# A Mamba2 scan with an ELU feed-forward layer on one core: where B's decay factor comes from, when block three and four are summed, and a last store in pieces

## The chip, the cores and the metric

The kernel runs on one core of a Trainium2 chip. The metric is the device time of one execution in microseconds (us), as the median of several executions. The core has these engines: PE (TensorE: matrix products, and PEld for its loads of weights), DVE (VectorE), ACT (ScalarE), POOL (GpSimd) and SP (SyncE, which here only issues DMAs). Each engine works through its own list of instructions in order and waits by semaphores for the others.

## The reference

Two computations follow each other. The first is a state-space scan (Mamba2), for 4 sequences of 768 tokens, 8 heads of width 32, and a state of width 16. For one chunk of tokens:

```python
cum = cumsum(log(clip(a, 1e-6, 1)))            # within the chunk
L   = exp(cum[:, None] - cum[None, :]) * causal
y   = (C @ B.T * L) @ x  +  (C @ state) * exp(cum)
state = exp(cum[-1]) * state + (B * exp(cum[-1] - cum)).T @ x
```

The heads of a token are then joined to a row of 256, which gives 3072 rows, and a feed-forward layer follows, `elu(y @ w_in) @ w_out`, from 256 to 2048 and back to 256. All is float32.

## The kernel before

**Blocks.** The 3072 tokens are cut into 12 blocks of 256, numbered n = 0 to 11 in the code. Block n is one third of one sequence. In the words of the change "block three" is n = 2 and "block four" is n = 3; below, blocks go by their n. In a block the scan works with four chunks of 64 tokens, written (u, v) with u and v in 0 and 1.

**The scan of a block.** `spread_cum(n)` (L348) loads the running sums from a table in DRAM that the kernel wrote before (`write_flat`), spread over the partitions. The exponential of these differences, by ACT (`decay_of` and `decay`, L481, with the token's own sum, `ncum`, as the bias), followed by POOL's causal select (L486), is the tile L: for a token j in the partition, a head, u, and a token i in the row, exp(cum_i - cum_j). Its last column, i = 63, is thus exp(cum_last - cum_j), the factor by which B is scaled before it is summed into the state. Before the change that factor is made on its own: `rest_of_sums` (L317) takes the differences to the last token on POOL (L299) and their exponential on ACT, and `turned` transposes it on PE and copies it on DVE to a tile `eb` (L961). `scaled(n)` (L374, the product is L379) multiplies B by it, on POOL; blocks 0 and 1 read an own tile eb0.

The rest of the scan is a list of steps with these lines. `turn` transposes B and C. `scores` (L501) multiplies C and B on PE, in four PSUM banks; `weigh` (L510) multiplies a bank by L on DVE and gives M. `sums` (L531) multiplies the scaled B and x on PE; `states` makes from it the state of each chunk on DVE (S_new, L548) and from each of these a masked copy on POOL (Sx, L553). `across` (L576, C by Sx) and `inside` (L595, M by x) are PE's products of block n's output y, which ACT copies to the tile yT (L612). In between, `ec`, the tile of exp(cum), is needed for C and for the states. Blocks 0 to 2 get it from `first_exp(n)` (L364: a product that picks heads by a mask from `make_heads`, L277, on POOL, and a copy on ACT), blocks 3 on from `spread_exp(n)` (L357), one load of 128 KB from a table in DRAM.

**The feed-forward layer.** `l1(n, i)` (L627) is the first product for block n and the i-th 256 of 2048 columns; with a second argument `parts` it is cut along the tokens, so that PE makes twice as many passes of half the width. `elu` follows it: e on ACT (L640), its exponential on ACT (L647), and g on DVE (L649), which frees the PSUM bank of the product. The products take turns in a pool of seven PSUM banks (an eighth is kept apart, p_o). `l2` (L748) is the second product for blocks 0 and 1. The weights come in 16 pieces (0 to 7 of w_in, 8 to 15 of w_out) of 512 KB. For a piece, `w_take` and `w_give` convert the words that the load brought: L174 (on ACT), L183, L192, L200 and L207 (on DVE), L217 (on POOL). A load of a piece is issued five or six pieces ahead.

From block 4 on, two blocks are worked on together. The products are combined from seven products of quarters in place of eight (`front`, `mid` and `back`, L699 to L732; `second`, L809, with sums of the products in L800, in c_sum). `second(n)` runs over two halves of the columns and over seven products r = 0 to 6 in each; `store(n, at)` (L852) writes one of the two blocks, 256 KB.

**The order.** Nothing schedules: what each engine does, and in which order, is the order in which the Python code calls these functions. Four stretches of it matter here.

- The start (L900 to L965): the first weights, blocks 0 and 1, and the first loads.
- A loop of twelve l1 for blocks 0 and 1, with s = 0 to 11 (L968 to L1006). Beside it run the decays of block 2 (s < 8), weight pieces 5 to 9 (at odd s), and the steps of block 2.
- Two rounds of eight l1 for n = 2 and 3, with i = 0 to 7 (L1087 to L1123). Beside them run the second products of blocks 0 and 1, pieces 10 to 15, and the scan of block 3; `scan_ahead(n, i)` (L1021) adds steps for blocks 4 and 5, and later for the blocks two ahead.
- The pairs from n = 4 on (L1127 to L1199), and the tail for blocks 10 and 11 (L1201 to L1212).

In the second of these, block 2 goes like this:

```python
        if s == 8:
            ...
            weigh(2, 2)
            weigh(2, 3)
            ...
            sums(2, 0, pool=p_o, tag="o", parts=(None, last))
            states(0, last)
            ...
            states(2)
        if s == 10:
            spread_cum(4)
            inside(across(2), 2)
```

Of the kernel before, what the change touches and what calls it, by code (L numbers as in the profile page):

```python
# [28 lines left out]
def kernel(  # L29
# [72 lines left out]
    def rows_of(n):  # L102
        b, g = place(n)
        return slice(NG * NH * b + g, NG * NH * (b + 1), NG)
# [165 lines left out]


    heads = [const.tile([P, NH, N], F32, name=f"heads{n}") for n in range(2)]
    heads.append(heads[0])

    def make_heads(n):
        cols = slice(BH + NH * n, BH + NH * (n + 1)) if n < 2 else rows_of(n)
        nc.gpsimd.tensor_copy(  # L277
            heads[n], ident[:, cols].unsqueeze(2).to_broadcast([P, NH, N]))

# [32 lines left out]
    nc.scalar.activation(E0, E0, ACT.Exp)  # L312

    F = const.tile([ROWS, 2, 2, P], F32, name="F")
    E = la

    def rest_of_sums():  # L317
        to_last(F[:, 0], E, nc.gpsimd)
        nc.scalar.activation(E, E, ACT.Exp)


    flat = tc.dram_tile([2, ROWS, 2, Q], F32, name="flat")
# [41 lines left out]
    def first_exp(n):  # L364

        ps = psum([P, 2, P], "ps_ec")
        rows = P if n < 2 else ROWS
        nc.tensor.matmul(
            out=ps, lhsT=heads[n][0:rows].rearrange("p h n -> p (h n)"),
            rhs=la0 if n < 2 else F[:, 1], start=True, stop=True)  # L370
        st[n]["ec"] = att.tile([P, 2, P], F32, tag="ec", name="ec", bufs=4)
        nc.scalar.copy(out=st[n]["ec"], in_=ps)

    def scaled(n, eng):  # L374

        s = st[n]
        s["sc"] = sc = att.tile([P, 2, NH, N], F32, tag="sc", name="sc", bufs=2)
        factor = eb0[:, :, NH * n:NH * (n + 1)] if n < 2 else eb[:, :, rows_of(n)]
        eng.tensor_tensor(  # L379
            out=sc, in0=s["b"] if n > 3 else s["bc"][:, 0],  # L380
            in1=factor.unsqueeze(3).to_broadcast([P, 2, NH, N]), op=ALU.mult)
# [91 lines left out]
    def decay(n, q):  # L473

        decay_of(n, 2 * q)
        decay_of(n, 2 * q + 1)
# [306 lines left out]

    c_of = {}

    def second(n):


        c = c_of[n] = ffn.tile([P, 2, 2, 2, P], F32, tag="c", name="c_sum", bufs=1)
        c11, c12, c21, c22 = (c[:, at, :, e] for e in range(2) for at in range(2))  # L790
        a11, a12, s1, a22 = a_out
        s2, s3, s4 = s_out
        for half in range(2):
            tmp = ffn.tile([P, 3, 2, P], F32, tag="tmp", name="p_sum", bufs=1)
            p1, p5, u = (tmp[:, r] for r in range(3))
            chunk = range(4 * half, 4 * half + 4)

            def add(out, in0, in1):
                eng = nc.vector if in0.tensor is ps.tensor else nc.gpsimd
                eng.tensor_tensor(out=out, in0=in0, in1=in1, op=ALU.add)  # L800

            for r, a in enumerate((a11, a12, s1, s2, s3, a22, s4)):
                pool, tag = (p_a, "a") if (7 * half + r) % 2 else (p_o, "o")
                ps = pool.tile([P, 2, P], F32, tag=tag, name="ps_o")
                for i in chunk:
                    b11, b21, b12, b22 = quarters(n, i)
                    b = (b11, b21, b12, t2_of[n, i], b11, b21, b22)[r]
                    for ts in range(2):
                        nc.tensor.matmul(  # L809
                            out=ps[:, ts], lhsT=b[:, ts * P:(ts + 1) * P], rhs=a[:, i],  # L810
                            start=(i == chunk[0] and ts == 0), stop=(i == chunk[-1]),
                            skip_group_check=True)
                    if i < chunk[-1]:
                        yield
                if r == 0:
                    nc.scalar.copy(out=p1, in_=ps)
                    for i in chunk:
                        b11 = quarters(n, i)[0]
                        sub(b11, t2_of[n, i], b11)
                    if half:  # L820
                        add(c11, c11, p1)
                elif r == 1:
                    add(c11, ps, c11 if half else p1)
                    for i in chunk:
                        b21 = quarters(n, i)[1]
                        sub(b21, b21, t2_of[n, i])
                elif r == 2:
                    nc.scalar.copy(out=p5, in_=ps)
                elif r == 3:
                    add(u, ps, p1)  # L830
                    add(p5, p5, u)
                    if half:
                        add(c22, c22, p5)
                        add(c12, c12, p5)
                elif r == 4:
                    add(c22, ps, c22 if half else p5)
# [86 lines left out]
    nc.scalar.activation(F[:, 1], F[:, 0], ACT.Exp)  # L923
    write_flat()
    spread_cum(2)
    w_load(5)
    load_bc(2)
    w_load(6)
# [11 lines left out]
    turn(1)  # L940
    first_exp(1)
    scaled(1, nc.gpsimd)
    rest_of_sums()
    w_give(3)
    make_heads(2)
    turn_exp(1)
    l1(0, 2)
    elu()
# [9 lines left out]
    inside(across(1), 1)  # L958
    w_take(4, nc.vector)
    ncum = turned(F[:, 0], "ncum", -1.0, nc.vector)  # L960
    eb = turned(E, "eb", 1.0, nc.vector)  # L961
    w_give(4)
    elu()
    load_bc(3)
# [3 lines left out]
    for s, (n, i) in enumerate((  # L968
            (1, 0), (1, 1), (1, 2), (0, 4), (1, 3), (0, 5), (1, 4), (0, 6), (1, 5), (0, 7),
            (1, 6), (1, 7))):  # L970
        l1(n, i, 2 if s < 2 else 1)
        if s < 8:
            decay_of(2, s)
        if s == 7:
            scores(2)
            weigh(2, 0)
            weigh(2, 1)
        if s % 2 == 1 and todo < 10:
            w_take(todo, nc.vector)
            w_give(todo)  # L980
            w_load(todo + 6)
            todo += 1
        if s == 4:
            scaled(2, nc.gpsimd)
        if s == 5:
            turn(2)
            first_exp(2)
            turn_exp(2)
        if s == 8:
            spread_cum(3)  # L990
            load_x(3)
            spread_exp(3)
            weigh(2, 2)
            weigh(2, 3)

            st[0] = kept
            sums(2, 0, pool=p_o, tag="o", parts=(None, last))
            states(0, last)
            st.pop(0)
            states(2)  # L1000
        if s == 10:
            spread_cum(4)
            inside(across(2), 2)
        if len(lag) > 1:
            elu()
# [15 lines left out]
    def scan_ahead(n, i):  # L1021
# [6 lines left out]
        if 4 <= m < NP and n % 2 == 0:  # L1028
            if i < 2:
                if m == 4:  # L1030
                    load_bc(m + i)
                spread_exp(m + i)
            if i == 2:
                if m == 4:
                    spread_cum(5)
                load_x(m)
                load_x(m + 1)
            for k in (i,) if m == 4 else (i, i + 1) if i % 2 == 0 else ():
                if k >= 2:
# [11 lines left out]
        if 4 <= m < NP and n % 2 == 1:  # L1051
            if i == 0:
                scaled(m, nc.gpsimd)
                scaled(m + 1, nc.gpsimd)
            for k in (i,) if m == 4 else (i, i + 1) if i % 2 == 0 else ():
                if k < 2:
                    decay(m + 1, k + 2)
            if i == 2 and m == 4:
                scores(m, m + 1)
                sums(m, m + 1)  # L1060
                for q in range(4):
                    weigh(m, q)
                    weigh(m + 1, q)
                states(m)
                states(m + 1)
# [21 lines left out]
    for n in (2, 3):  # L1087
        for i in range(8):
# [13 lines left out]
            if n == 2:  # L1102
# [3 lines left out]
                if i == 1:  # L1106
                    scaled(3, nc.gpsimd)
                    turn(3)
                    turn_exp(3)
                if i == 2:  # L1110
                    scores(3)
                    for q in range(4):
                        weigh(3, q)
                if i == 4:
                    sums(3)
                    states(3)
                if i == 6:
                    inside(across(3), 3)
# [80 lines left out]
    next_elu()  # L1199

    n = NP - 2  # L1201
    steps = second(n)
    for k in range(56):
        if k == 1:
            store(n - 2, 0)
            store(n - 2, 1)
        if k == 54:
            store(n, 0)
        next(steps)
    for _ in steps:  # L1210
        pass
    store(n, 1)  # L1212


# [28 lines left out]
```

## Time and profile before

| | |
|---|---|
| median of 3 executions | 357.79 us (357.79 to 358.67) |
| the profiled execution, its own time | 357.64 us |
| its span in the profile | 355.9 us |
| granted clock of PE, mean | 0.998 |
| DMA | 26.36 MB, mean 74 GB/s |
| L809, PE's second products of pairs (`w_out` by g), 640 passes | 81.0 us, mean 275 ns |
| L627, PE's `l1`, 272 passes | 60.9 us, mean 371 ns |
| L699, PE's products of pairs (yT by `w_in`), 128 passes | 38.8 us, mean 385 ns |
| L640 and L647, ACT's e, 96 of each | 57.0 and 60.9 us, means 593 and 635 ns |
| L649, DVE's g, 96 | 65.1 us, mean 679 ns |
| L486, POOL's causal select, 40 | 28.8 us, mean 719 ns |

The first two times are of whole executions; the span is from the first to the last instruction that the profiler saw, and so a little shorter than the execution that it belongs to. A row of a chain or of an order in time starts with the start and the length in us; then come engine, line, operation, the tile written and the tiles read (out<-in), their sizes, a count where equal instructions are drawn together, and in brackets the idle time of the engine before it and what ended that. An engine may be busy for most of the span and still bound nothing: what sets the time is the chain of work that ends last.

### The profile page before, as it was taken

The numbers are of one execution on the slowest core, as the hardware profiler recorded it, in microseconds if no ns is written. First come the engines' busy times: TensorE is split into PE (matmuls) and PEld (weight loads), VectorE is DVE, ScalarE is ACT, GpSimd is POOL, SyncE is SP. The second block draws the span as 40 slices with busy tenths as digits, with TensorE's granted clock in tenths as the row PEclk, the third lists the DMA queues.
The fourth block names the chain that finished last, engine by engine and source line by source line (L and its number), as shares of the span: only waits on it lengthen the run. The fifth ranks groups of instructions, "written<-read, shape, count | busy, mean of one in ns | idle before, by whom it ended". The sixth has DMA issues, their size and how long they took to land.

```text
span 355.9 us, 9943 instructions
## 1 busy us (share of the span) xinstructions
PE 349.0 (98%) x3962; PEld 313.4 (88%) x3962; DVE 242.5 (68%) x500; ACT 200.5 (56%) x491; POOL 231.8 (65%) x367
## 2 busy tenths in 40 slices
PE   8899999999999999999999999999999999999995
PEld 5579888888888999899999899999899999999995
DVE  3999987993999768674677684677674555656212
ACT  4759969867425577535577535576635544444000
POOL 5553643663676997869477769477769444464973
PEclk9999999999999999999999999999999999999999
DMA  8978998470460500146500145600000100000001
GB/s 156 209 195 155 246 318 174 96 122 31 72 139 2 120 0 3 19 98 132 113 0 2 17 102 112 133 3 0 2 2 4 59 3 0 2 0 33 29 2 60
DMA packets 82742, 26.36 MB, mean 74 GB/s; under 512 B 59720, under 2 KB 78600, under 8 KB 82696
## 3 DMA queue, kind: packets, MB, share of 16 engines
q1 hardware_dynamic: 80520, 25.53, 32.2%
q8 instruction: 31, 0.51, 0.6%
q10 hardware_dynamic: 2176, 0.20, 0.5%
q14 instruction: 15, 0.12, 0.1%
HBM read 22.38 MB, written 3.34 MB: 72 GB/s over the span
## 4 chain that ended last, share of the span: by engine, by line
PE 93%; DVE 3%; ACT 1%; POOL 1%; issue 0%; POOLq 0%; DVEq 0%
PE ps_o L809 35%; PE ps_h L699 28%; PE ps_h L627 14%; PE ps_o L748 8%; PE ps_y L595 2%; PE ps_g L501 2%; PE ps_y L576 1%; PE ps_st L531 1%; PE ps_idle L232 1%; DVE mag L207 1%; DVE mag L200 1%; DVE M L510 1%; DVE sgn L192 0%; DVE g L649 0%; POOL w_in L217 0%; ACT L L471 0%
## 5 line engine op out<-in xcount | busy, mean ns | idle before, releaser
L640 ACT ACTIVATE e<-ps_h 128x512 f32<-128x512 f32 x96 | 57.0, 593 | 89.5 <-DVE ps_h L724 44.0
L809 PEld LDWEIGHTS ps_o<-w_out,g 128*128 128x128 f32 x640 | 79.9, 192 | 3.1 <-issue 0.5
L809 PE MATMUL ps_o<-w_out,g 128*128 128x128 f32 x640 | 81.0, 275 | 0.0
L649 DVE SCALAR_TENSOR_TENSOR g<-e,ps_h 128x512 f32<-128x512 f32 x96 | 65.1, 679 | 10.5 <-ACT e L647 10.4
L627 PE MATMUL ps_h<-yT,w_in 128*128 128x256 f32 (+1 forms) x272 | 60.9, 371 | 1.7 <-POOL w_in L217 1.7
L647 ACT ACTIVATE e<-e 128x512 f32<-128x512 f32 x96 | 60.9, 635 | 2.0
L776 POOL TENSOR_TENSOR g<-g 128x256 f32<-128x256 f32 x33 | 23.9, 726 | 54.4 <-DVE g L649 54.4
L627 PEld LDWEIGHTS ps_h<-yT,w_in 128*128 128x128 f32 x272 | 48.4, 190 | 9.5 <-POOL w_in L217 3.1
L809 PE MATMUL ps_o<-w_sum,g 128*128 128x128 f32 x320 | 42.9, 275 | 0.0
L809 PEld LDWEIGHTS ps_o<-w_sum,g 128*128 128x128 f32 x320 | 41.1, 192 | 1.2
L481 ACT ACTIVATE L<-L,ncum 128x64 f32<-128x64 f32 x160 | 41.0, 337 | 0.0
L699 PE MATMUL ps_h<-yT,w_in 128*128 128x256 f32 x128 | 38.8, 385 | 0.0
L732 DVE TENSOR_TENSOR ps_h<-ps_h,u_sum 128x512 f32<-128x512 f32 x32 | 22.3, 698 | 23.5 <-PE ps_h L699 23.4
L699 PE MATMUL ps_h<-y_sum,w_in 128*128 128x256 f32 x128 | 38.1, 380 | 0.0
L699 PE MATMUL ps_h<-y_sum,w_sum 128*128 128x256 f32 x128 | 38.1, 380 | 0.0
L486 POOL TENSOR_SCALAR_AFFINE_SELECT L<-L 64x512 f32<-64x512 f32 x40 | 28.8, 719 | 10.8 <-ACT L L481 9.5
L716 DVE TENSOR_TENSOR u_sum<-ps_h,u_sum 128x512 f32<-128x512 f32 x32 | 22.1, 689 | 14.5 <-ACT u_sum L709 8.1
L724 DVE TENSOR_TENSOR ps_h<-ps_h,u_sum 128x256 f32<-128x256 f32 x32 | 13.8, 432 | 26.3 <-PE ps_h L699 26.3
L748 PE MATMUL ps_o<-w_out,g 128*128 128x256 f32 x128 | 30.8, 384 | 0.0
L764 POOL TENSOR_TENSOR t<-g 128x256 f32<-128x256 f32 x40 | 28.9, 756 | 0.3
L764 POOL TENSOR_TENSOR g<-g,t 128x256 f32<-128x256 f32 x40 | 28.8, 752 | 0.3
L764 POOL TENSOR_TENSOR g<-t,g 128x256 f32<-128x256 f32 x40 | 27.9, 730 | 1.1 <-PE ps_o L809 1.1
(111 smaller groups left out, 533.9 us busy)
## 6 DMA issues: line engine op xcount, KB each, us to landing
L<-flat SPq DMA_DIRECT2D x20, 256.0 KB
w<-in_moe_w_in_dram SPq DMA_DIRECT2D x8, 512.0 KB
w<-in_moe_w_out_dram SPq DMA_DIRECT2D x8, 512.0 KB
xr<-in_x_dram SPq DMA_DIRECT2D x24, 128.0 KB
out_dram<-c_sum SPq DMA_DIRECT2D x10, 256.0 KB
bc<-in_B_dram SPq DMA_DIRECT2D x24, 64.0 KB
bc<-in_C_dram SPq DMA_DIRECT2D x22, 64.0 KB
ec<-flat_exp SPq DMA_DIRECT2D x9, 128.0 KB
```

The source lines that it names most:

```text
L481: nc.scalar.activation(L[:, h, u], L[:, h, u], ACT.Exp, bias=ncum[:, u, row:row + 1])
L486: nc.gpsimd.affine_select(out=part, in_=part, pattern=[[0, 4], [0, 2], [1, Q]], compare_op=ALU.is_ge, fill=0.0, base=0, channel_multiplier=-1)
L627: nc.tensor.matmul(out=ps[:, j, toks], lhsT=w_in[:, k, m * P:(m + 1) * P], rhs=yT[n // 2][:, k, n % 2].rearrange("p u i -> p (u i)")[:, toks],
L640: nc.scalar.activation(begun[0], lag[0][2], ACT.Relu, scale=-1.0)
L647: nc.scalar.activation(e, e, ACT.Exp, scale=-1.0)
L649: nc.vector.scalar_tensor_tensor(out=g_of[n, i], in0=e, scalar=1.0, in1=ps, op0=ALU.subtract, op1=ALU.max)
L699: nc.tensor.matmul(out=out, lhsT=lhsT, rhs=rhs, start=first, stop=True, skip_group_check=True)
L732: nc.vector.tensor_tensor(out=c2, in0=c2, in1=u[:, 0:2], op=ALU.add)
L748: nc.tensor.matmul(out=o_of[n][:, ts], lhsT=g_of[n, j][:, m % 2, ts * P:(ts + 1) * P], rhs=w_out[:, m], start=(m == 0 and ts == 0), stop=( ...
L764: nc.gpsimd.tensor_tensor(out=out, in0=in0, in1=in1, op=ALU.subtract)
L776: eng.tensor_tensor(out=b12, in0=b12, in1=b11, op=ALU.subtract)
L809: nc.tensor.matmul(out=ps[:, ts], lhsT=b[:, ts * P:(ts + 1) * P], rhs=a[:, i], start=(i == chunk[0] and ts == 0), stop=(i == chunk[-1]), s ...
```

## The change

- **The factor of B.** `rest_of_sums`, the tile `eb` and its transposes go. `scaled(n)` for n from 2 on reads `L[:, :, :, Q-1]`. `scaled(2)` moves from s = 4 to s = 7, behind the last decay.
- **ec of block 2.** `first_exp(2)` and the mask `make_heads(2)` go; `spread_exp(2)` is loaded, issued on SP right behind `spread_cum(2)` and ahead of weight piece 5, B and C of block 2, piece 6, x of block 2, and pieces 7 to 9.
- **Block 2.** `sums(2)` and the states move from s = 8 to s = 9, where they come behind `w_take(9)` and `w_give(9)` in the code; `inside(across(2))` moves from s = 10 to s = 11. The l1 at s = 2 is cut in halves, as those at s = 0 and 1 were.
- **Block 3.** `scores(3)` (before at i = 2) and `sums(3)` (before at i = 4) stand together at i = 3, ahead of `weigh`. The states stay at i = 4.
- **Later blocks.** `decay` comes two steps earlier for the pairs from m = 6 on, so that L is there for `scaled`; for block 5 `scaled` comes one step later.
- **The tail.** In the last half of `second(10)` the last of seven products is cut in two along the tokens. Each half has a PSUM tile, a sum of 128x128 on DVE, and a store of 64 KB of its own. The other 128 KB of block 11 are stored at k = 53, together with the store of block 10 (before at k = 54); the store of all of block 11 at the end goes.

```diff
-    heads.append(heads[0])
     def make_heads(n):
-        cols = slice(BH + NH * n, BH + NH * (n + 1)) if n < 2 else rows_of(n)
+        cols = slice(BH + NH * n, BH + NH * (n + 1))
...
-    E = la
-    def rest_of_sums():
-        to_last(F[:, 0], E, nc.gpsimd)
-        nc.scalar.activation(E, E, ACT.Exp)
...
     def scaled(n, eng):
-        factor = eb0[:, :, NH * n:NH * (n + 1)] if n < 2 else eb[:, :, rows_of(n)]
+        factor = (eb0[:, :, NH * n:NH * (n + 1)] if n < 2 else
+                  s["L"][:, :, :, Q - 1].rearrange("p h u -> p u h"))
...
     def second(n, final=False):
...
             for r, a in enumerate((a11, a12, s1, s2, s3, a22, s4)):
+                if final and half and r == 6:
+                    for ts in range(2):
+                        ps = psum([P, P], "ps_o")
+                        for i in chunk:
+                            nc.tensor.matmul(
+                                out=ps, lhsT=quarters(n, i)[3][:, ts * P:(ts + 1) * P],
+                                rhs=a[:, i], start=(i == chunk[0]), stop=(i == chunk[-1]))
+                            if i % 2:
+                                yield
+                        part = c12[:, ts]
+                        nc.vector.tensor_tensor(out=part, in0=ps, in1=part, op=ALU.add)
+                        r0 = row_of(n + 1) + ts * P
+                        nc.sync.dma_start(out=out[r0:r0 + P, 0:P], in_=part)
+                    continue
...
     spread_cum(2)
+    spread_exp(2)
     w_load(5)
...
     scaled(1, nc.gpsimd)
-    rest_of_sums()
     w_give(3)
-    make_heads(2)
...
-    eb = turned(E, "eb", 1.0, nc.vector)
...
-        l1(n, i, 2 if s < 2 else 1)
+        l1(n, i, 2 if s < 3 else 1)
         if s < 8:
             decay_of(2, s)
+        if s == 7:
+            scaled(2, nc.gpsimd)
         if s == 7:
             scores(2)
...
-        if s == 4:
-            scaled(2, nc.gpsimd)
         if s == 5:
             turn(2)
-            first_exp(2)
             turn_exp(2)
         if s == 8:
...
             weigh(2, 3)
-
+        if s == 9:
             st[0] = kept
             sums(2, 0, pool=p_o, tag="o", parts=(None, last))
...
         if s == 10:
             spread_cum(4)
+        if s == 11:
             inside(across(2), 2)
...
-            for k in (i,) if m == 4 else (i, i + 1) if i % 2 == 0 else ():
-                if k >= 2:
-                    decay(m + k // 6, (k - 2) % 4)
+            if m > 4 and i % 2 == 0:
+                decay(m + i // 4, i % 4)
+                decay(m + i // 4, i % 4 + 1)
+            elif m == 4 and i > 1:
+                decay(m + i // 6, (i - 2) % 4)
...
             if i == 0:
                 scaled(m, nc.gpsimd)
+            if m == 4 and i < 2:
+                decay(m + 1, i + 2)
+            if i == (1 if m == 4 else 0):
                 scaled(m + 1, nc.gpsimd)
-            for k in (i,) if m == 4 else (i, i + 1) if i % 2 == 0 else ():
-                if k < 2:
-                    decay(m + 1, k + 2)
...
-                if i == 2:
+                if i == 3:
                     scores(3)
+                    sums(3)
                     for q in range(4):
                         weigh(3, q)
                 if i == 4:
-                    sums(3)
                     states(3)
...
-    steps = second(n)
+    steps = second(n, True)
     for k in range(56):
...
-        if k == 54:
+        if k == 53:
             store(n, 0)
+            r0 = row_of(n + 1)
+            nc.sync.dma_start(
+                out=out[r0:r0 + BLK, P:2 * P].rearrange("(t p) c -> p t c", p=P),
+                in_=c_of[n][:, 1, :, 1])
         next(steps)
     for _ in steps:
         pass
-    store(n, 1)
```

More of the change, by code (lines that the diff above doesn't have):

```diff
@@ L366, in first_exp @@
         ps = psum([P, 2, P], "ps_ec")
-        rows = P if n < 2 else ROWS
         nc.tensor.matmul(
-            out=ps, lhsT=heads[n][0:rows].rearrange("p h n -> p (h n)"),
-            rhs=la0 if n < 2 else F[:, 1], start=True, stop=True)
+            out=ps, lhsT=heads[n].rearrange("p h n -> p (h n)"), rhs=la0, start=True, stop=True)
         st[n]["ec"] = att.tile([P, 2, P], F32, tag="ec", name="ec", bufs=4)
@@ L784, with second @@
     c_of = {}
-    def second(n):
+    def second(n, final=False):
         c = c_of[n] = ffn.tile([P, 2, 2, 2, P], F32, tag="c", name="c_sum", bufs=1)
```

## The prediction

> **What bounds the kernel now.** I read the page first, for the busy shares, then the chain of waits over the span and in its first 53 us, then the order in time of the engines in the stretches that the change touches, and last a table of stretches for the tail.
>
> ```profile
> span 355.9 us, 9943 instructions
> ...
> PE 349.0 (98%) x3962; PEld 313.4 (88%) x3962; DVE 242.5 (68%) x500; ACT 200.5 (56%) x491; POOL 231.8 (65%) x367
> ...
> PE 93%; DVE 3%; ACT 1%; POOL 1%; issue 0%; POOLq 0%; DVEq 0%
> ```
>
> PE is busy in 98% of the span and carries 93% of the chain, so a wait taken away counts only where PE stands still, and a new wait of PE counts in full. From 53 us to 352 us the chain is PE almost without a break. What can move is the start (0 to 53 us) and the tail (352 us on). The chain around block 2, in order of time (start, length):
>
> ```profile
> 39.13 0.43 PE ps_ec L368 x2
> 39.57 3.46 PE ps_h L627 x16
> 43.02 0.62 PE ps_g L501 x32
> 43.65 1.92 PE ps_h L627 x8
> 45.57 0.59 PE ps_st L531 x40
> 46.16 3.65 PE ps_h L627 x16
> 49.81 0.42 PE ps_y L576 x32
> 50.22 0.81 PE ps_y L595 x53
> 51.04 1.94 PE ps_h L627 x8
> ```
>
> Here PE runs without a gap. Beside it DVE, ACT and POOL, from their order in time:
>
> ```profile
> 34.68 0.69 ACT L174 ACTIVATE mag<-w 128x512 f32<-128x512 f32 x1 [0.36 <-DMA w<-in_moe_w_in_dram]
> ...
> 42.79 0.69 DVE L649 SCALAR_TENSOR_TENSOR g<-e,ps_h 128x512 f32<-128x512 f32 x1
> 43.76 0.76 DVE L510 TENSOR_TENSOR M<-ps_g,L 128x256 f32<-128x256 f32 x2 [0.28 <-PE ps_g L501]
> ...
> 47.55 1.54 DVE L548 SCALAR_TENSOR_TENSOR S_new<-S_new,ec,ps_st 128x64 f32<-128x64 f32 x5
> ```
>
> and on POOL:
>
> ```profile
> 48.10 1.36 POOL L553 TENSOR_TENSOR Sx<-S_new,hmask 128x64 f32<-128x64 f32 x5
> 51.50 1.26 POOL L217 TENSOR_TENSOR w_out<-mag,w_out 128x512 uint32<-128x512 uint32 x1 [2.04 <-DVE mag L207]
> ```
>
> DVE has no gap from 43.76 to 52.02. The states of block 2 (S_new, Sx) are made just in time for the products at 49.81, and before weight piece 9, whose words end on POOL with the row at 51.50. ACT waits at 34.68 for weight piece 6. The end of the kernel, as a table of stretches:
>
> ```profile
> 353.50:354.00 0.50, 0.00 (x0) 0.00 (x0) 0.00 (x0) 0.00 (x0) 0.00 (x0) 1.00 1.03 346
> 354.00:354.50 0.50, 0.00 (x0) 0.00 (x0) 0.00 (x0) 0.00 (x0) 0.00 (x0) 0.80 0.49 162
> ```
>
> The last sum of c ends at 352.51 on DVE; the last 256 KB move until about 354.25 (last two columns: DMA share, GB/s), and the span ends at 355.9.
>
> **What the skill says.** "SBUF — State Buffer", Who interferes with whom: DVE and GpSimd share a pair of ports, taken by a DVE instruction in a two-port mode or with two SBUF inputs; the other waits. The trace agrees: mag L200 takes 0.42 us at 50.28 with POOL idle, and 0.81 at 20.52 beside POOL's L299. "DMA: Bandwidth & Descriptors", Anatomy of one DMA: the fixed cost is mostly the receipt at the end. Here 1.6 us pass from the last data (354.25) to the end of the span, which smaller stores don't shorten. The same page, Issuing engines are not separate DMA queues: all transfers use the same 16 engines, so a load put ahead delays those behind it. DMA share is 0.99 to 1.28 from 24 to 28 us, which fits.
>
> **The change, part by part.**
>
> Sums of the rest (L317) and third mask (L277). Removed: POOL 0.60 and 0.29, ACT 0.42. ACT's e at 21.41 can start when the copy of ec ends, 20.60. mag L200 no longer runs beside POOL: 0.41 for 0.81, so piece 3 is whole 0.4 earlier and the l1 that waits for it starts at 23.12 for 23.53. DVE's S_new follow at about 24.0 for 24.54, the products at 25.05 for 25.58. PE gains 0.5 us by 27.76.
>
> eb (L961). Two transposes, 0.17 us of the chain at 27.58. The next product waits for ACT's yT until 27.71 anyway: nothing. DVE saves 0.35.
>
> first_exp(2). PE saves 0.43 (39.13 row), ACT a copy of 0.38 less overlap plus 0.16 idle: 0.43. In its place is one load, below.
>
> Third l1 in halves: 16 passes at 0.111 us (L809: 16 in 1.78) for 8 at 0.216 (1.73): +0.05.
>
> So PE could reach scores(2) 0.5 + 0.43 - 0.05 = 0.9 us earlier. I expect it not to. By the built program the l1 of s = 8 needs the PSUM bank that g of s = 5 frees. That g ends at 43.48 now, 0.1 before the product; it hangs on ACT, which runs without another pause than 0.16 from the wait at 34.68 to 42.76. The new load is queued on SP ahead of weight pieces 5 and 6, block 2's B and C, and x. Its issue is 0.6 us (L360: 590 ns least, 1.28 most), its 128 KB take 0.4 to 0.5 us at the 250 to 326 GB/s of 24 to 27 us. I take 0.45 for the delay of piece 6 (0.1 if the half idle DMA engines of 28 to 32 us swallow it, 1.0 if it blocks SP for the longest issue). ACT's exp of s = 5: 42.76 - 0.43 + 0.45 = 42.78. DVE gets there with g of s = 4 at 42.85, then g of s = 5 until about 43.5. PE resumes l1 at 43.6 as now: the 0.9 us turn into a wait for a bank.
>
> Block 2's sums one step later, products two lines later. scaled(2) moves from 38.97 to behind the last select, about 44.75 to 45.45 on POOL; sums at s = 9 don't wait for it. But L548's five instructions now stand behind w_take(9) and w_give(9) on DVE, and Sx behind piece 9's addition on POOL. From M at 43.7, start to start: M 0.67, piece 8's words 1.86, g 0.59, M 0.67, g 0.66, piece 9's words 1.82, hand-over 0.1, POOL's addition 1.27, three Sx at 0.27 = 0.81. That is 8.45: 52.15. scaled(2) now runs beside piece 8's sgn and mag (0.41 each; beside POOL up to 0.88): I add 0.4 (0 to 0.5). So block 2's products start at 52.55. PE arrives at 43.6 + 1.92 + 1.73 + 0.59 + 3.65 = 51.5, and waits about 1.05. They take 0.42 + 0.81, so l2(0,0) starts at 53.8 and, with the 0.2 that the first product behind such a burst costs (1.94 against 1.73), ends at 55.75; now it starts at 52.98 and ends at 54.71. Loss: 1.05 us (0.2 to 1.7). Queued behind the waiting product is all of PE; ACT's yT copies (1.65) then hide behind l2(0,0) by 0.3.
>
> scores and sums of block 3 in one burst: apart they cost 0.62 + 0.2 and 0.38 + 0.2; in one the second 0.2 goes. Gain 0.19.
>
> M of block 3 behind piece 13; and ACT, where e and exp follow the yT copies, runs some 0.7 us later relative to PE: pieces 11 and 12 keep 0.2 us in hand against about 1.2 and 0.1 now, and the l1 behind the burst waits for the g before it (six banks are taken). I take 0.3 us of new stalls (0 to 0.7).
>
> decay two steps earlier in the later blocks, scaled reading L there: eight ACT instructions (2.0 us) at i = 0 instead of later. They delay the first e by 1.1 us; two of seven banks are free then and POOL waits 54.4 us in all for g (L776), so nothing shows. scaled(5) one step later leaves 0.3 us. Nothing.
>
> Last store in pieces. PE's products stay equal. The last sum is 128x128: about 0.28 (between 128x64 at 0.22 and 128x256 at 0.42), 0.14 less. SP issues take 0.385 each; three stand between 350.95 and 352.1, so the last issues at once. It moves 64 KB in about 0.25 us for 0.75. Gain 0.65 (0.4 to 0.85).
>
> Sum: +1.05 - 0.19 + 0.3 - 0.65 = +0.5 us. The profiled execution took 357.64 (span 355.9, 1.7 around it): 358.15. The median of the runs shown is 357.79, 0.15 above it, so it is 358.2.
>
> **Rivals.**
> Faster: piece 6 isn't late (0.1), DVE keeps 0.35 of its lead, POOL's scaled(2) costs DVE nothing and nothing stalls later. Block 2's products then cost 1.05 - 0.35 - 0.4 - 0.3 = 0; -0.19 - 0.85 remain and the 0.07 that PE waits for piece 14 at 75.3 goes: -1.1, 356.5. For it: DMA share is only 0.24 to 0.67 from 29 to 32 us. Against: ACT's wait at 34.68 shows that the piece comes late already.
> Slower: block 2's states behind piece 9 on DVE and POOL, at their dear end. With piece 6 late by 1.0 (+0.55), contention 0.5 (+0.1), stalls 0.7 behind it (+0.4) and 0.5 at the tail (+0.15): +1.7, 359.4. It decides from products of block 2 that start after 53.1 us. For it: no gap in DVE for 8 us. Against: each term must be at its end.
> A third: the load is hidden and the bank isn't the limit, but the states still wait; that lands between 357.1 and 357.9, inside my forecast.
>
> **How the numbers follow.** 0.3% is 1.07 us, about what can be told from no change here. Forecast (no change, 356.8 to 358.8): 0.45. Faster (355.7 to 356.7): 0.28. Slower (358.9 to 360.2): 0.27. The range reaches into both rivals until about 0.1 below and 0.1 above are left out: 356.1 to 359.5. The forecast's own range is 356.8 to 358.8.
>
> **What would show it.** PE's first product of yT<-block 2 at 52 to 53 us with a wait for Sx or g; l1 of s = 8 near 43.6 with a wait for g; L174 for piece 6 near 35.1; the last DMA issue near 352.4 and the span's end about 3.2 us behind the last product, where it is 3.8 now. It is wrong if PE reaches block 2's products at 51 us without a wait, or if a PE wait over 0.5 us appears after 116 us.

## The result

The changed kernel takes 359.49 us (median of 11 executions, 358.61 to 360.4); the kernel before took 358.29 us beside it (11 executions, 357.51 to 358.86). The ratio is 1.0034, with a 95% interval of 1.0019 to 1.0049: the change costs about 1.2 us, 0.34%. The forecast was 358.2 us, no change that can be measured, with a range of its own from 356.8 to 358.8; the time lies 0.7 us above that range, at the very edge of the wider one of 356.1 to 359.5, and in the range of the rival that had the change slower (358.9 to 360.2).

The profiled execution of the changed kernel took 360.06 us, and that of the kernel before 357.64. Their difference, 2.4 us, is larger than that of the medians, because the one before was a short execution of its kind and the one after a long one. Below, a place is read from these two traces, and its weight from the medians and from other kernels that share the program up to that place.

### The profile page after: what moved, and what is told of

Its sections match the earlier page's. It is cut to its first block, busy times and chain, and to the rows that moved or that the text cites. A ratio compares the mean times of both kernels' runs of the same rounds, so it can differ in the third digit from the quotient of the medians.

```text
span 358.3 us, 9940 instructions
## 1 busy us (share of the span) xinstructions
PE 349.1 (97%) x3966; PEld 313.5 (87%) x3966; DVE 239.5 (67%) x500; ACT 199.9 (56%) x489; POOL 231.4 (65%) x365
## 4 chain that ended last, share of the span: by engine, by line
PE 86%; DVE 4%; POOL 3%; SPq 2%; DMA 2%; issue 1%; ACT 1%; POOLq 0%
PE ps_o L816 35%; PE ps_h L692 27%; PE ps_h L620 9%; PE ps_o L741 8%; PE ps_y L588 2%; SPq L129 2%; DMA w<-in_moe_w_in_dram 2%; POOL w_in L217 2%; PE ps_g L494 1%; PE ps_y L569 1%; PE ps_st L524 1%; DVE mag L207 1%; DMA bc<-in_C_dram 1%; DVE sgn L192 1%; DVE mag L200 1%
## 5 line engine op out<-in xcount | busy, mean ns | idle before, releaser
L816 PE MATMUL ps_o<-w_sum,g 128*128 128x128 f32 x304 | 40.9, 275 | 0.0
L816 PEld LDWEIGHTS ps_o<-w_sum,g 128*128 128x128 f32 x304 | 39.2, 192 | 1.2
L479 POOL TENSOR_SCALAR_AFFINE_SELECT L<-L 64x512 f32<-64x512 f32 x40 | 27.8, 695 | 12.0 <-ACT L L474 8.2
```

The source lines that it names most:

```text
L479: nc.gpsimd.affine_select(out=part, in_=part, pattern=[[0, 4], [0, 2], [1, Q]], compare_op=ALU.is_ge, fill=0.0, base=0, channel_multiplier=-1)
L816: nc.tensor.matmul(out=ps[:, ts], lhsT=b[:, ts * P:(ts + 1) * P], rhs=a[:, i], start=(i == chunk[0] and ts == 0), stop=(i == chunk[-1]), s ...
```

## The profile after

First the page of the changed kernel: span, busy times, and the chain's shares by engine.

```profile
span 358.3 us, 9940 instructions
...
PE 349.1 (97%) x3966; PEld 313.5 (87%) x3966; DVE 239.5 (67%) x500; ACT 199.9 (56%) x489; POOL 231.4 (65%) x365
...
PE 86%; DVE 4%; POOL 3%; SPq 2%; DMA 2%; issue 1%; ACT 1%; POOLq 0%
```

PE is busy for as long as before (349.1 for 349.0 us), and the span is 2.4 us longer: all of the loss is PE standing still. DVE and ACT have less to do (3.0 and 0.6 us less), which buys nothing. The chain no longer runs over PE alone. Where it leaves PE, in order of time (start, length):

```profile
50.14 0.70 DVE mag L207
...
50.91 1.27 POOL w_out L217
52.18 0.76 POOL Sx L546 x3
...
52.98 0.71 PE ps_y L569 x32
53.70 0.81 PE ps_y L588 x54
54.51 1.92 PE ps_o L741 x8
```

These are the words of weight piece 9 on DVE, their addition on POOL, three of block 2's Sx behind it, and then PE's products of block 2. Before, the same products came at 49.81, with one `l1` between them and the first `l2`; that `l2` started at 52.98, and it now starts at 54.51. The waits of PE, as the profile lists them (in all, times, longest):

```profile
PE ps_y L569 <- POOL Sx L546: 1.1, 1, 1.1
...
PE ps_g L494 <- DVE ctm L389: 0.2, 1, 0.2
PE ps_h L620 <- DVE g L642: 0.2, 1, 0.2
```

The second and third are what became of the 0.7 us by which PE comes earlier to block 2's scores (42.29 for 42.95): they wait for DVE, and the `l1` behind them for a PSUM bank, until 43.95. What else stands ahead of the states on DVE, from the order in time of all engines:

```profile
35.62 0.69 ACT L174 ACTIVATE mag<-w 128x512 f32<-128x512 f32 x1 [0.66 <-DMA w<-in_moe_w_in_dram]
...
44.55 0.85 DVE L183 TENSOR_SCALAR w_out<-w 128x512 f32<-128x512 uint32 x1
...
45.20 0.69 POOL L372 TENSOR_TENSOR sc<-bc,L 128x256 f32<-128x256 f32 x1
...
45.32 0.86 DVE L192 TENSOR_SCALAR sgn<-w 128x512 uint32<-128x512 uint32 x1
```

Piece 6 is 0.94 us later than before (34.68). L183 takes 0.85 us for 0.55 and L192 0.86 for 0.41, beside POOL's select and the new place of `scaled(2)`: 0.75 us more in all.

Farther on, PE's lag on the kernel before grows from 1.53 us at the first `l2` to 1.98 at 116 us. Of that, 0.2 us is the first product behind a burst, which before fell to the `l1` ahead of that `l2`. The burst of block 3 gives back 0.12; an `l2` at 65.5 loses 0.16 and an `l1` at 72.13 0.26. From 137 to 140 us 0.30 more are lost, by a chain through three engines:

```profile
136.99 0.42 DVE L793 TENSOR_TENSOR c_sum<-ps_o,p_sum 128x256 f32<-128x256 f32 x1 [1.30 <-POOL p_sum L793]
...
139.28 0.69 DVE L709 TENSOR_TENSOR u_sum<-ps_h,u_sum 128x512 f32<-128x512 f32 x1
...
140.02 0.30 PEld L692 LDWEIGHTS ps_h<-y_sum,w_sum 128*128 128x128 f32 x2 [0.43 <-DVE u_sum L709]
```

POOL makes two selects of the earlier decays at 126.08 (1.39 us) that it made later before, and has no gap from there on, so that its p_sum ends at 136.96; before it ended at 133.15, which with the lag is 1.8 us earlier. DVE waits 1.30 us for it, so the sums and e of this step come late, and PE waits 0.43 us. Then the lag stays at 2.28 to 2.40 us until the end. The tail, in the order in time of DVE and SP:

```profile
353.78 0.47 SPq L1217 DMA_DIRECT2D out_dram<-c_sum  x1
354.37 1.22 SPq L808 DMA_DIRECT2D out_dram<-c_sum  x2
354.48 0.29 DVE L806 TENSOR_TENSOR c_sum<-ps_o,c_sum 128x128 f32<-128x128 f32 x1 [0.60 <-PE ps_o L800]
```

and the last store by itself, in the kernel before and in the changed one:

```profile
352.54 0.37 SPq L852 DMA_DIRECT2D out_dram<-c_sum  x1
...
355.23 0.35 SPq L808 DMA_DIRECT2D out_dram<-c_sum  x1
```

The last sum ends at 354.77, the issue of its store starts at 355.23, and by the records of the DMA packets its data move from 356.08 to 356.60, so they end 1.83 us after the sum. Before, these times were 352.51, 352.54, and 353.43 to 354.38: 1.87 us. (The prediction's 354.25, and the 1.74 and 1.73 us in an expectation below, were read from tables of half microseconds.) The sum is 0.13 us shorter and its data take 0.52 us for 0.96, but the issue starts 0.46 us after the sum for 0.03, and the end comes 1.74 us after the data for 1.55. The span ends 4.18 us after the last product's start, before 4.16. The pieces gain nothing here.

## The experiments

All ratios are against the kernel before, in executions on the same chip, with a 95% interval. The changed kernel stands at 1.0034 (1.0019 to 1.0049).

**The order of block 2 alone.** The kernel before, with one edit:

```diff
             weigh(2, 3)
+        if s == 9:
             st[0] = kept
             sums(2, 0, pool=p_o, tag="o", parts=(None, last))
...
         if s == 10:
             spread_cum(4)
+        if s == 11:
             inside(across(2), 2)
```

> The kernel before with one edit of the change: sums and states of block 2 at s = 9 behind piece 9, and its products at s = 11. Theory: a wait of PE for Sx near 53 us, and 1.2 us more than before (0.8 to 1.6). Rival (the loss needs the new load as well, or scaled in its new place): less than 0.4 us more.

Measured: 359.1 us, ratio 1.0034 (1.0021 to 1.0047). The wait for Sx is there (0.58 us), and the products start at 51.85. This one edit costs what the whole change costs. It needs neither the new load nor `scaled` in its new place. The trace loses more behind the products than in them: from the first `l2` to the products of blocks 4 and 5 it takes 57.79 us for 57.22. All kernels of this document together have four lengths for this stretch: 57.22 to 57.24 us with block 2 at its old place and block 3 as before (seven kernels), 57.03 to 57.04 with block 2 at its old place and block 3's burst (five), 57.57 to 57.62 with the late block 2 and the burst (four, the changed kernel among them), and 57.79 here. So the late place costs 0.55 us behind the start of the first `l2`, of which 0.2 is the dear first product, now on the other side of that start; and the burst gives 0.19 back.

**The states ahead of piece 9, in the changed kernel.** The five lines of `if s == 9:` are put ahead of `w_take(9)`:

```diff
+        if s == 9:
+            st[0] = kept
+            sums(2, 0, pool=p_o, tag="o", parts=(None, last))
+            states(0, last)
+            st.pop(0)
+            states(2)
         if s % 2 == 1 and todo < 10:
             w_take(todo, nc.vector)
...
-        if s == 9:
-            st[0] = kept
-            sums(2, 0, pool=p_o, tag="o", parts=(None, last))
-            states(0, last)
-            st.pop(0)
-            states(2)
```

> The changed kernel with the sums and states of block 2 put ahead of weight piece 9 at s = 9, everything else as changed. Theory (the states stand behind the words of piece 9 on DVE and POOL): S_new starts near 48.5 us in place of 50.75, PE's first product of block 2 near 51.9 without a wait in place of 52.98 with 1.07, and the time falls by 1.1 to 1.5 us against the changed kernel, to about the kernel before. Rival (the PSUM bank, or a load that comes late, limits PE anyway): PE waits elsewhere by 54 us and less than 0.4 us is won.

Measured: 359.12 us, ratio 1.0037 (1.0022 to 1.0052). Nothing is won, and the theory in this form fell. From the order in time of this kernel:

```profile
48.87 1.54 DVE L541 SCALAR_TENSOR_TENSOR S_new<-S_new,ec,ps_st 128x64 f32<-128x64 f32 x5
...
52.16 1.28 DVE L642 SCALAR_TENSOR_TENSOR g<-e,ps_h 128x512 f32<-128x512 f32 x2
...
52.90 0.45 PE L569 MATMUL ps_y<-cts,Sx 32*64 32x64 f32 x20 [0.87 <-DVE g L642]
```

S_new is early (48.87, as expected), and PE begins the products at 51.67, but after twelve of them it needs a PSUM bank that a g frees, and that g is now behind piece 9 on DVE. DVE has the same work ahead of the products in either order. What moved is their place: at s = 11 they stand behind one more `l1`, whose g DVE reaches only after piece 9.

**Block 2 at its old places, in the changed kernel** (the first edit above, reversed).

> The changed kernel with block 2's steps at their old places: sums and states at s = 8 ahead of piece 9, products at s = 10. Theory (the place of the products matters, since at s = 11 they stand behind one more l1 and wait for either Sx or a g that are behind piece 9 on DVE): no wait of PE over 0.4 us at these products, about 1.0 us less than the changed kernel (0.7 to 1.4), so within 0.3 us of the kernel before. Rival (DVE and ACT are late anyway because of the new load, so a wait moves to the l1 behind the products): less than 0.4 us is won.

Measured: 359.19 us, ratio 1.0021 (1.0007 to 1.0035). By the ratios about a third of the loss is gone, though the intervals overlap. No wait for Sx or g is left at the products. In its place, from the waits and the chain of this kernel:

```profile
PE ps_y L588 <- issue: 0.8, 1, 0.8
```

```profile
50.66 0.65 PE ps_y L588 x45
...
52.14 0.35 PE ps_y L588 x13
```

PE stops in the middle of L588 for 0.83 us, and the profile names no one that it waits for. What this kernel wins is the 0.55 us behind the first `l2` (its stretch takes 57.04 us); what it doesn't win back lies ahead of that and behind. The same gap stands in the profiled execution of three kernels that are, up to here, the kernel before (0.65 us with the changed tail, 0.34 with the early decays, 0.18 with block 3's burst). It is taken up below.

**The load later.** `spread_exp(2)` is moved from ahead of `w_load(5)` to behind `w_load(6)`, in the changed kernel, and in the changed kernel with the old places.

```diff
     spread_cum(2)
-    spread_exp(2)
     w_load(5)
     load_bc(2)
     w_load(6)
+    spread_exp(2)
     load_x(2)
```

> The changed kernel with the load of ec of block 2 issued behind weight piece 6 in place of ahead of piece 5. Theory: piece 6 is there about 0.9 us earlier, L174 for it starts near 34.7 us in place of 35.62, M of block 2 and the states follow by 0.5 to 0.9 us, and so the time is 0.5 us less than the changed kernel (0.3 to 0.9). Rival (the wait is set by DVE's work from 43.9 us on, whatever came before): L174 is earlier but less than 0.2 us is won.

> Both: block 2's steps at their old places, and the load behind piece 6. If the two causes add, 1.4 us less than the changed kernel (1.0 to 1.9), 0.2 to 0.5 below the kernel before. If the old places alone take the whole wait away, the same as with the old places within 0.2 us.

Measured: 359.81 us, ratio 1.0040 (1.0026 to 1.0054), and 359.45 us, ratio 1.0022 (1.0006 to 1.0037). Nothing is won in either. L174 for piece 6 starts at 35.15 and 34.58, but the wait for Sx is 1.07 us as in the changed kernel, and the gap in L588 is there as with the old places alone. By these two runs the place of the load gains nothing.

**The later decays alone**, in the kernel before (the diff of `scan_ahead`, without the lines of `scaled`).

> The kernel before with the decays of the later blocks two steps earlier, as changed, and B's factor as before. Theory from the trace of the changed kernel (0.43 us between two products at 140.02, and 0.1 us more near 163): 0.3 to 0.4 us more than before, between the products of blocks 4 and 5 near 110 us and the scores near 146 us. Rival (the step of the prediction): nothing within 0.1 us there.

Measured: 358.53 us, ratio 1.0013 (1.0000 to 1.0026). From the products of blocks 4 and 5 to the scores of the next pair it takes 36.52 us for 36.23, with the gap at 138.60 us: 0.29 us, in the place and of the size that the changed kernel shows. Of the kernels without added instructions, all seven with the early decays have 36.49 to 36.53 there and all six without 36.22 to 36.23. The ratio alone would not show it, since its interval begins at 1.0000.

**The tail**: the changed kernel with the old one, the kernel before with the new one, and the latter with its first 64 KB store issued by ACT:

```diff
-                        nc.sync.dma_start(out=out[r0:r0 + P, 0:P], in_=part)
+                        (nc.sync if ts else nc.scalar).dma_start(
+                            out=out[r0:r0 + P, 0:P], in_=part)
```

> The changed kernel with the last product and the stores as before. Theory from the trace of the changed kernel (four stores stand in SP's queue, and the last data end 1.73 us after the last sum, as before with 1.74): no difference within 0.2 us. Rival (the step of the prediction): 0.65 us slower, 0.4 to 0.85.

> The kernel before with the changed tail alone. Theory (SP's queue): within 0.2 us of before, the span ends 3.7 to 4.0 us behind the last product. Rival (the step of the prediction): 0.65 us faster, the span ends about 3.2 us behind the last product.

> The kernel before with the changed tail, its first 64 KB store issued by ACT. Theory: 0.2 to 0.3 us less than before, since the span ends 5.6 us behind the start of the last product in place of 5.8 to 5.9. Rival: 0.6 us less, as the prediction had it.

Measured: 359.22 us, ratio 1.0034 (1.0017 to 1.0050); 357.81 us, ratio 0.9994 (0.9982 to 1.0006); 358.13 us, ratio 0.9997 (0.9982 to 1.0012). From the start of the last product to the end of the span it takes 4.10 us with the old tail in the changed kernel, 3.99 and 3.97 with the new ones on the kernel before, and 3.93 to 4.19 over all kernels with the old tail. The new tail gains nothing that can be told from the spread, and a second queue adds nothing. In all ten kernels with the new tail the issue of the last store starts 0.37 to 0.49 us after the last sum, in all seven with the old one 0.03. With the second queue it is 0.39, though SP's issue before it had ended 0.5 us ahead of the sum, so SP's queue isn't what the small stores lack. Why the issue starts late is not shown.

**Block 3's burst alone**, in the kernel before: `scores(3)` and `sums(3)` at i = 3.

> The kernel before with block 3's scores and sums in one burst at i = 3, as changed. Theory from the changed kernel's trace (0.19 us of one burst less, against 0.16 us in an l2 near 65.5 and 0.26 us in an l1 near 72 that waits for piece 12): within 0.3 us of before, most likely 0.1 to 0.2 more. Rival (the step of the prediction, with 0.3 us of stalls and 0.19 won): 0.1 more; the two can be told apart only by where the gaps stand in the trace.

Measured: 358.21 us, ratio 1.0000 (0.9987 to 1.0012). The stretch behind block 2 is 0.19 us shorter, and neither of the two gaps near 65 and 72 us is there. The two kernels with the burst and the old places of block 2 have the same short stretch (57.03 and 57.04 us). So these gaps belong to the changed kernel's lateness at block 2, not to the burst.

**The factor and the load alone**: block 2 and 3, the split `l1`, the decays and the tail as before, with `scaled(n)` one step later for every second later block, since its decays come late.

> The kernel before with the new factor of B and the load of ec of block 2 alone: block 2 and 3, the decays, the split l1 and the tail stay as before (for every second later block B is scaled one step later). Theory: PE is ahead by 0.4 to 0.9 us until the products of block 2 and loses it there, because it must wait for the fetch of its next 256 instructions, which ends near 50 us whatever PE does: within 0.4 us of the kernel before, with a gap over 0.5 us in L588. Rival (scaled beside piece 8 and the late piece 6 cost DVE enough): 0.5 us or more slower, with a wait for g or Sx at block 2.

Measured: 360.61 us, ratio 1.0074 (1.0050 to 1.0098). The first part went as expected: PE is 0.9 us ahead at 26.85 us, stands in L588 until 51.17, and reaches the first `l2` at 53.41 for 52.98. The rest of the loss comes from `scaled` one step later. From the waits of this kernel:

```profile
PE ps_st L524 <- POOL sc L372: 1.9, 3, 0.8
```

Three pairs of blocks wait for `scaled`, 0.8 to 1.0 us between two products each, since L must be complete before its last column is read. So the earlier decays, which cost 0.3 us, are what the new factor needs: without them, in this form, it costs about 2 us.

**The gap without a name.** The PE instructions come by DMA: the page has 31 packets on the queue q8 (kind: instruction, 0.51 MB), 16 KB each, and PE has 8021 records in the trace of the kernel before, 259 for each packet. Counted in records from the start, the gap in L588 or L595 stands at 1473 in all six kernels that show it. The DMA records give the end of the fifth packet (us):

```
                                    5th packet ends   PE goes on at   later by
kernel before                          49.17            50.67 (no gap)  1.50
before, early decays                   49.85            51.27           1.42
before, block 3's burst                50.39            52.00           1.61
factor and load alone                  49.65            51.17           1.52
before, new tail                       50.32            51.91           1.59
changed, old places                    50.66            52.14           1.48
changed, old places, load later        50.38            51.84           1.46
```

To test it, 48 PE instructions were added at the very start of the kernel before (to see whether the gap follows the count or the work), of the changed kernel with the old places, of that with the decays in their old order and `scaled` one step later, and of the kernel before with the tail of two queues:

```diff
-    idle_product(4)
-    idle_product(3)
+    for _ in range(14):
+        nc.tensor.matmul(
+            out=ps_idle[:, 0, 0:64], lhsT=idle, rhs=idle[:, 0:64], start=True, stop=True)
```

> The kernel before with 48 more PE instructions at the very start: the two idle products there, 896 columns in all, become fourteen of 64 columns. No computed value changes. Theory (in some executions of the kernel before PE stands in the products of block 2 until 1.4 to 1.6 us after the fetch of its next 256 instructions): the place of the fetch in the program moves 48 instructions ahead, it starts 1 to 3 us earlier, no gap over 0.3 us in L595 near 51 us, executions spread by less than the 1.3 us of before, and a median 0.3 to 0.7 us lower. Rival (the gap has another cause): nothing within 0.2 us, and gaps in the same products.

> The changed kernel with block 2's steps at their old places and the same 48 instructions more at the start. Theory (after the old places the gap of 1.04 us in L588 was the fetch): the gap goes, 0.7 to 1.0 us less than with the old places alone, about the time of the kernel before. Rival: as with the old places alone within 0.2 us.

> As the one before, and the later decays in their old order, with B scaled one step later for every second block. Theory: the gap of 0.41 us near 139 us goes, 0.3 to 0.4 us less than the one before, 0 to 0.4 below the kernel before. Rival: scaled one step later costs PE elsewhere and nothing is won.

> The kernel before with 48 more PE instructions at the start and the changed tail, whose first 64 KB store is issued by ACT instead of SP. Theory (in the changed tail the last store waits in SP's queue behind three others): the last issue starts within 0.1 us of the last sum, the span ends 3.3 to 3.5 us behind the last product's end in place of 3.8, so 0.3 to 0.5 us less than the kernel before with the 48 instructions alone. Rival (the receipt of the last store sets it, not the queue): 0 to 0.15 us.

Measured: 367.52 us, ratio 1.0241 (1.0201 to 1.0280); 368.36 us, 1.0249 (1.0211 to 1.0287); 370.11 us, 1.0332 (1.0301 to 1.0362); 366.25 us, 1.0219 (1.0189 to 1.0249). As a way to be faster all four fell. The fourteen small products take 6.24 us for 3.35 (28 passes at 0.22), and the loop's first product comes 3.8 us later. Most of the rest is new gaps, and they show what the gap follows. In the first kernel:

```profile
PE ps_y L596 <- issue: 3.1, 2, 1.8
...
PE ps_h L700 <- issue: 1.5, 1, 1.5
```

The three gaps stand at the records 1473, 5569 and 6850, with 1.44, 1.92 and 2.06 us between two products. The first is 24 products earlier in the program than in the kernel with the changed tail, and at the same count. The distances are 4096 and 5377, 16 times 256 and 21 times 256 with 1 over. In the second kernel gaps stand at 961, 3010, 5569 and 6850, and in the fourth at 3010, 5569 and 6850, with a small one at 961: all on the same grid of 256, within one record. At 5569 and 6850 in these three PE goes on 1.22 to 1.45 us after the end of a packet. So the gap follows the count and not the work. In all 17 profiles, with a gap or without, PE begins record 1473 at least 1.28 us after the end of the fifth packet. That PE waits for the fetch of its next 256 instructions fits all of this; no run changes the fetch alone.

In the traces the first kernel is 10.9 us longer than the kernel before (spans of 366.8 and 355.9 us; 9.5 in the medians). Of that, 3.8 us come at the start, 5.4 in the three gaps, and 1.7 behind the last gap, where the granted clock of PE is 0.5 for 3.4 us, from 281.16 on (the last three columns are the clock, the DMA share and GB/s):

```profile
282.00:284.00 2.00, 2.00 (x9) 1.82 (x8) 0.85 (x2) 0.39 (x1) 1.70 (x3) 0.50 0.00 0
```

Each of these four kernels has one or two such stretches, of 3.41 us, that begin 0.3 to 1.3 us after PE goes on behind one of its gaps; not every gap has one behind it. The third kernel has three more gaps of 0.8 to 1.0 us at `sums`, which wait for `scaled`, as the kernel with the factor alone.

No kernel was clearly faster than the kernel before.

## Why the prediction was right and wrong

**Right.** The start: the loop's first product came 0.56 us earlier (0.5 predicted). That the 0.9 us would turn into a wait for a bank: the `l1` of s = 8 resumed at 43.95 (43.6), with the wait for g. The products of block 2 at 52.98 (52.55), waiting 1.07 us (1.05) for Sx behind piece 9. The stalls around block 3, 0.42 us (0.3), and the burst's gain, 0.19 us alone (0.19).

**Sized wrong.** Piece 6 was 0.94 us late for 0.45 (0.1 to 1.0); the runs with the load moved show that this decides nothing. DVE lost 0.75 us beside POOL for 0.4, more than the 0.5 that was put as the most. The first `l2` came at 54.51 for 53.8: 0.43 from the start of the products, and 0.29 because L569 waits on for the last two Sx (0.71 for 0.42).

**The steps that failed.** First, the tail: the gain of 0.65 us, which took away more than half of block 2's 1.05, is nothing that the runs can tell (3.93 to 4.23 us from the start of the last product to the end, over both tails). The step said that the last store issues at once and that its 64 KB take 0.25 us for 0.75. The trace has the issue 0.46 us after the sum, where the large store had 0.03, and the data in 0.52 us for 0.96. So the 0.57 us that the shorter sum and the data save go into the later issue (0.43) and the later end behind the data (0.19). Nor is most of a store's fixed part at its end, as the prediction had it from a section on DMAs that GpSimd issues, where these are SP's: before, 0.89 us pass from the start of the last issue to the first data, and 0.6 from the last data to the last notice of landing.

Second, the decays: the step set the time that they delay against PE's free banks and against the 54.4 us that POOL waits in all for g, and said that nothing shows. But that is a sum over the whole span, and not slack at this place. In the trace of before, the first of these waits ends at 143.7 us, and POOL has no gap of more than 0.15 us from 121.3 to 139 (the first column behind the comma is POOL's busy time):

```profile
121.30:139.00 17.70, 17.17 (x27) 1.00 0.01 1
```

POOL's selects move with the decays into this stretch, ahead of POOL's p_sum: 0.3 us, shown alone. With the tail at nothing and the decays at 0.3, the sum of the prediction would have been +1.45 us for +0.5, where the medians show +1.2. Its three times also don't count from one base: from the median of 357.79 its sums give 358.3 for the forecast, 356.7 and 359.5 for the rivals.

**The place, not the state order, is what costs.** The prediction priced the states behind piece 9. Putting them ahead of it gave nothing back, since at s = 11 the products wait for a g in the same queue. Its rival "slower" had the right side and nearly the time (359.4), and two of its dear ends nearly came true in the trace: piece 6 (0.94 us for 1.0) and DVE beside POOL (0.75 for 0.5); the products began at 52.98, just short of its sign of 53.1. But an earlier piece 6 won nothing, the stalls were 0.42 us for 0.7, and it too had 0.5 us for the tail and nothing for the decays, so that its time came out is in part luck.

**The point of reference.** Five kernels share the program up to block 2's products and one `l1` more. In their profiled executions the first `l2` has its first record at 52.82, 53.37, 53.62, 54.01 and 54.10 us, on average at 53.58; the trace that the prediction was worked from is the earliest, and in the last, with block 3's burst, PE's granted clock was 0.5 for 3.4 us from 14.46 on. It had no gap at record 1473 because the fetch had ended 1.50 us before PE came there, just early enough. In the four kernels with the start of the change and the products of block 2 at s = 11 the first `l2` is at 54.09, 54.20, 54.44 and 54.83, on average 0.8 us later. That agrees with the 1.05 of the prediction no better than it can: single executions of one program differ by 1.3 us here, and in the kernel with the late block 2 alone, which costs 1.1 us in the medians, it is at 53.31.

What stays open: why the fifth packet comes when it does (it ends between 49.1 and 50.7 us in all kernels without added instructions, while the DMA share is about 1.0), why the small last store is issued late, and how the two thirds of the loss divide that the old places didn't give back. An estimate from the traces: 0.3 us for the decays, 0.5 ahead of the first `l2` (54.25 and 53.95 us in the two kernels with old places, for 53.58), less 0.19 for the burst, which makes 0.6 of the 0.75 us in the ratios. In these two kernels PE comes to record 1473 early and stands 1.0 to 1.1 us there, so the lead that the new start gives is lost there.

## What to carry to other kernels

Before a consumer is moved one step back in a PE queue, look at what it will then wait for in every form, operands and banks alike; if both come from one full engine, reordering that engine's work only changes the name of the wait. When something is made earlier, follow all engines that make it, at the place where it will run: a wait that is summed over the span says nothing of the room there, and here ACT had room and POOL hadn't. A store's time is worth splitting into issue, start, data and receipt before a gain is booked on its size, and one profile is worth comparing with another of the same program before 1 us is read from it.

## What the runs showed of the hardware

PE's instruction stream arrives in 16 KB packets (31 for 8021 records, one for each 256 or so), and by the count of the gaps PE can run into the end of it. Many small products do that: the products of block 2 are 192 records (96 products and their loads) in 1.2 us. PE went on 1.22 to 1.61 us after the end of a packet in every gap on the grid that was looked at. The profile shows such a wait as "issue", without a releaser, in the middle of a group of equal products; it can be known by its count, which stays on a grid of 256 while the work under it shifts. Adding 48 instructions at the start moved gaps of about 2 us into the bursts at 224 and 279 us, where the kernel before has none.

A store of 64 KB at the end, in rows of 512 bytes, took 0.37 to 0.59 us for its data where 256 KB in rows of 1024 took 0.89 to 0.97, and its issue started 0.37 to 0.49 us after the sum that it waits for, in ten kernels, where the larger store's started 0.03 after, in seven.
